# An order written out by hand, re-made: half-height products in one group, two spectra formed in other ways, convolution by row pairs

## The chip, the core and the metric

The kernel runs on one core of one Trainium2 chip. The core has a matrix engine (PE, with the loading of its stationary operand shown apart as PEld), three engines for element-wise work (DVE, ACT, POOL) and one that only starts transfers (SP). They run side by side, each through its own list of instructions in order, and wait for each other by semaphores. SP and POOL start nearly all transfers, so a transfer also waits for whatever stands ahead of it in their lists. The metric is the device time of one execution in microseconds; lower is better.

## The reference

Two layers follow each other on 2048 tokens of width 640, in bf16.

```
h  = x + q' * (irfft(rfft(kv) * rfft(ssm_k)) + kv * ssm_D)     # first 2048 samples of a length-4096 convolution
     q' = layernorm(x),  kv = v * (k filtered with 4 taps along the tokens)
h2 = h + (silu(n @ w_gate) * (n @ w_up)) @ w_down,   n = layernorm(h),  w_gate, w_up: 640 x 1728
```

So each channel is convolved with a filter as long as the sequence, and a gated feed-forward layer (FFN) follows. 1728 is 13 chunks of 128 and one chunk of 64.

## The kernel before

The 2048 tokens are cut into four blocks of 512 (block 0 to 3). A block is laid out with four tokens per partition: partition p holds tokens 4p to 4p+3, and "row r" is the 128 tokens 4p+r.

The long convolution is done block against block with transforms of length 1024. For each block j there is

- a short filter (`kv_of`): taps as diagonal matrices, multiplied on PE. For blocks 1 to 3, k lies in a buffer `T`, transposed by DMA and copied so that one product takes two taps (64 output columns each, 20 products for each row r, 80 for a block, line L648). The three copies inside `T` (`load_two`) are transfers and ACT copies. The result is multiplied by v to give kv.
- a spectrum X of kv and a spectrum G of the filter's block (`transform`, products at L375 with the basis `WF`; 128 x 320 each, two for a width of 640). The half of the frequencies comes from the even rows, the other from the odd rows: `hi = twice the even part - lo` is a subtraction on DVE (L410). In the form "four" (`SUM`) the rows are split once more, by n mod 4: half as many products, but more sums on DVE (L439, L443). In the form "direct" (`DIRECT`, only G of block 0) the difference is made on PE with a second, negated basis that is loaded into `tT` (`const_minus`).
- a window H from two neighbouring G (`window`, and `window_of` for the last block), the complex products X[i] * H[j-i] summed over i (`mac`: four multiplications and two additions for the first pair of a block, four and four for each further one; L719, L746, L747), and the way back (`inverse`, L823 to L858 on DVE, L878 on PE).
- two layer norms. `ln1` (of x) and the second norm take sums on ACT (L757, L796); the rest (`norm`: mean, variance, inverse root) is a run of tiny instructions, on POOL for `ln1` of every block and for the second norm of blocks 1 and 2, on DVE for the second norm of blocks 0 and 3. `h = x + (x-m)*s*y` is one fused instruction on DVE from PSUM (L892) and an addition (L905, or an accumulating transfer).
- the transposed rows hT for the FFN: on PE for block 0, by DMA from SP for blocks 1 to 3 (`turn_h`, L919).

The FFN of a block (`ffn`) has 27 products of 5 x 128x512 for gate and up (L1022, evicted by ACT at L1012 and L1014, multiplied on DVE at L1016, L1034 and L1039) and then, row by row, 14 chunks x 2 halves of 128x320 with `w_down` (L1110). The 14th chunk has only 64 features; it is padded with zeros to 128. Rows of blocks 0 to 2 are copied out of PSUM by ACT (L1116) and added to the output by a transfer; those of block 3 are added to h on DVE (L1125, L1127).

Additions of two big tiles can be done by DVE or by an accumulating transfer that POOL starts (`add_into`, L278). The names in `ADDLO`, `ADDWIN`, `ADDH`, `ADDP`, `ADDINV` say which.

Nothing of the sequence follows from loops. Every step is recorded as a numbered operation, and the list `ORDER` gives the order in which all operations are emitted; a negative number takes the operation's alternative engine. Buffers are taken from fixed pools in that order:

```python
SLOTS = {'S': 8, 'big': 12, 'kT': 0, 'tT': 1, 'row': 5, 'sg': 0, 'co': 2, 'ps': 4, 'sm': 6}
...
        for n in order:
            op = self.ops[n if n >= 0 else ~n]
            ...
            for b in op.bufs:
                if b.tag is not None and b.at is None:
                    b.at = idle[b.tag].pop(0)
```

There are thus four PSUM tiles (`ps`, two banks each) and twelve large tiles (`big`) for everything, the FFN's weights among it.

In the order before, the FFN of block j-1 fills PE while the convolution of block j keeps DVE busy; the FFN of block 3 stands alone at the end.

Of the kernel before, what the change touches and what calls it, by code (L numbers as in the profile page):

```python
# [17 lines left out]
D = 640  # L18
# [13 lines left out]
ADDLO = ('G1', 'G2', 'X1', 'X2', 'X3')  # L32
ADDMAC = ()
ADDWIN = (1,)
ADDH = (1, 2)
LEAD = {}
PAD = 16
DIRECT = ('G0',)
# [8 lines left out]
SUM = {'X3': 'four', 'i2': 'four', 'i3': 'four', 'G3': 'four'}  # L47
ADDP = {(1, 1): ((0, 1),)}
ADDINV = (2,)
# [9 lines left out]
KVPAIR = ()  # L59
DPOOL = False  # L60
# [54 lines left out]
def make_basis():  # L115
# [14 lines left out]
    minus = np.stack([(wf[:, r].astype(np.float32) * -2).astype(bf) for r in (1, 3)] + [-wi[:, :, r].reshape(P, 4 * P) for r in (1, 3)], axis=1)  # L130
    return wf.reshape(P, R, 4, P), wi, np.ascontiguousarray(minus)

class Buf:
# [76 lines left out]
def kernel(ctx: ExitStack, tc: tile.TileContext, A_q, A_k, A_v, A_shift_k, A_ssm_k, A_ssm_D, B_x,  # L213
# [493 lines left out]
    def mac(A, X, H, first, pieces=((0, 1),), adds=(), at=None):  # L707
# [26 lines left out]
        if first:  # L734
            return
# [595 lines left out]
```

## Time and profile before

| | us |
|---|---|
| median of 3 runs | 261.12 |
| lowest, highest | 260.46, 261.9 |
| span of the profiled execution, first to last instruction | 259.6 |
| PE busy, DVE busy, ACT busy, POOL busy | 251.3, 198.6, 180.0, 97.0 |
| granted TensorE clock | 1.0 throughout |
| moved by DMA | 45.38 MB |

For the profiled execution itself only its span is given; the runs' median lies 1.5 us above it. "Busy" is the time in which at least one instruction of the engine is under way. For PE this includes the time a product takes to leave the array, so back-to-back products count as one stretch. The start of one product to the start of the next is read from the chain or the timeline, where runs of equal products are merged with their count.

### The profile page before, as it was taken

The page shows a single profiled execution, that of the slowest core. Times are in us where ns is not written, and L with a number is a line of the kernel's source. Part 1 is how long each engine was busy: PE and PEld are TensorE (multiplying, and loading weights), DVE is VectorE, ACT ScalarE, POOL GpSimd, SP SyncE. Part 2 cuts the span into 40 slices and gives each one's busy share as a digit, 9 for nine tenths or more (in the row PEclk, how much of TensorE's full clock was granted, in tenths as well). Part 3 has the DMA queues.
Part 4 walks back from the last instruction along what each step waited for, and adds up shares of the span by engine and source line. Part 5 has one row for each costly group of instructions (what it writes and reads, how often), then busy time and mean ns, then how long its engine had stood idle before and what let it go on. Part 6 is the DMA issues. An engine that isn't in the chain of part 4 may idle for free.

```text
span 259.6 us, 4700 instructions
## 1 busy us (share of the span) xinstructions
PE 251.3 (97%) x1803; PEld 154.2 (59%) x1818; DVE 198.6 (77%) x259; ACT 180.0 (69%) x297; POOL 97.0 (37%) x115
## 2 busy tenths in 40 slices
PE   8999899999998999999999999999999999999994
PEld 7967577654654477754465477544456764444663
DVE  4679999999998999999999999999998200004403
ACT  2899999999998998569855985655497134637200
POOL 7961300008914199926117962240951022000000
PEclk9999999999999999999999999999999999999999
DMA  6997999979999998999997965994498546000002
GB/s 218 403 251 119 289 252 340 280 115 279 247 238 168 182 217 204 190 191 201 214 231 110 299 151 107 198 238 130 100 215 255 101 77 70 8 0 0 13 15 76
DMA packets 64752, 45.38 MB, mean 175 GB/s; under 512 B 31014, under 2 KB 60267, under 8 KB 64731
## 3 DMA queue, kind: packets, MB, share of 16 engines
q1 hardware_dynamic: 58896, 32.96, 51.1%
q0 software_dynamic: 5824, 12.13, 24.9%
q8 instruction: 14, 0.23, 0.4%
q14 instruction: 8, 0.06, 0.1%
q10 hardware_dynamic: 10, 0.01, 0.0%
HBM read 30.01 MB, written 4.59 MB: 133 GB/s over the span
## 4 chain that ended last, share of the span: by engine, by line
PE 78%; ACT 9%; DMA 6%; DVE 2%; issue 2%; SPq 1%; ACTq 0%; DVEq 0%
PE ps L1022 40%; PE ps L1110 23%; PE ps L375 10%; DMA big<-in_B_w_up_dram 4%; PE ps L878 3%; DMA big<-in_A_q_dram 3%; ACT T L565 2%; ACT big L364 1%; ACT S L364 1%; PE ps L648 1%; ACT row L757 1%; ACT big L664 1%; ACT big L473 1%; ACT tT L1014 1%; DVE row L892 1%
## 5 line engine op out<-in xcount | busy, mean ns | idle before, releaser
L1022 PE MATMUL ps<-big,big 128*128 128x512 bf16 x525 | 119.9, 379 | 1.7 <-DMA big<-in_B_w_up_dram 0.8
L1022 PEld LDWEIGHTS <-big 128*128 128x128 bf16 x540 | 52.5, 98 | 61.1 <-DMA big<-in_B_w_up_dram 1.3
L1110 PE MATMUL ps<-wd,tT 128*128 128x320 bf16 (+1 forms) x416 | 60.3, 299 | 0.0
L1110 PEld LDWEIGHTS <-tT 128*128 128x128 bf16 x416 | 40.7, 98 | 16.3
L1016 DVE TENSOR_TENSOR tT<-tT,co 128x2048 bf16<-128x2048 bf16 x12 | 14.5, 1219 | 34.4 <-ACT tT L1014 32.4
L375 PE MATMUL ps<-big,WF 128*128 128x320 bf16 x240 | 39.1, 299 | 1.3 <-ACT big L364 1.0
L1012 ACT CAST co<-ps 128x1024 bf16<-128x1024 f32 x24 | 24.2, 1011 | 17.3 <-PE ps L1022 16.8
L747 DVE TENSOR_TENSOR S<-S,big 128x2560 bf16<-128x2560 bf16 x23 | 34.3, 1492 | 1.2 <-DMA S<-big 0.5
L746 DVE TENSOR_TENSOR big<-S,S 128x2560 bf16<-128x2560 bf16 x23 | 34.1, 1485 | 0.2
L375 PEld LDWEIGHTS <-WF 128*128 128x128 bf16 x240 | 23.1, 97 | 12.8 <-issue 2.3
L1014 ACT ACTIVATE tT<-ps 128x1024 bf16<-128x1024 f32 x24 | 24.5, 1029 | 8.8 <-PE ps L1022 8.7
L757 ACT ACTIVATE row<-big 128x640 bf16<-128x640 bf16 x32 | 23.5, 742 | 1.8 <-DMA big<-in_A_q_dram 1.1
L807 ACT ACTIVATE row<-big,sm 128x640 bf16<-128x640 bf16 x23 | 20.3, 922 | 3.8 <-POOL sm L789 2.8
L1117 POOL DMA_DIRECT2D out_dram<-row x12 | 11.8, 1010 | 29.2 <-ACT row L1116 29.1
L364 ACT CAST S<-ps 128x320 bf16<-128x320 f32 (+1 forms) x36 | 19.4, 583 | 0.3
L1116 ACT CAST row<-ps 128x640 bf16<-128x640 f32 x12 | 8.1, 691 | 14.2 <-PE ps L1110 13.2
L364 ACT ACTIVATE big<-ps 128x640 bf16<-128x640 f32 (+1 forms) x24 | 15.6, 696 | 0.7 <-PE ps L375 0.7
L278 POOL DMA_DIRECT2D big<-row x8 | 7.0, 919 | 22.9 <-DVE row L892 22.9
L892 DVE SCALAR_TENSOR_TENSOR row<-row,ps 128x640 bf16<-128x640 bf16 x16 | 12.8, 815 | 1.1 <-PE ps L878 0.9
L278 POOL DMA_DIRECT2D S<-big x2 | 2.5, 1266 | 26.3 <-DVE S L719 19.1
L719 DVE TENSOR_TENSOR big<-S,S 128x2560 bf16<-128x2560 bf16 (+1 forms) x10 | 12.2, 1218 | 0.1
L959 POOL DMA_DIRECT2D big<-in_B_w_gate_dram x8 | 9.1, 1137 | 8.1 <-PE ps L1022 7.8
(110 smaller groups left out, 330.4 us busy)
## 6 DMA issues: line engine op xcount, KB each, us to landing
big<-in_B_w_up_dram SPq DMA_DIRECT2D x17, 320.0 KB, 5.1
big<-in_B_w_gate_dram SPq DMA_DIRECT2D x16, 320.0 KB, 4.7
big<-in_A_ssm_k_dram SPq DMA_DIRECT2D x4, 640.0 KB, 9.2
big<-in_A_q_dram SPq DMA_DIRECT2D x4, 640.0 KB, 7.6
big<-in_A_v_dram SPq DMA_DIRECT2D x4, 640.0 KB, 6.9
big<-in_B_w_gate_dram POOLq DMA_DIRECT2D x8, 320.0 KB, 7.2
big<-in_B_w_up_dram POOLq DMA_DIRECT2D x7, 320.0 KB, 6.7
wd<-in_B_w_down_dram SPq DMA_DIRECT2D x1, 2080.0 KB, 12.2
```

The lines of the kernel that those rows point to most:

```text
L364: (lambda: nc.scalar.activation(dst(), src(), ACT.Copy, scale=2.0)) if twice else (lambda: nc.scalar.copy(dst(), src())),
L375: nc.tensor.matmul(ap(ps)[:, h, 0:NH], w, ap(src)[:, r, h * NH:(h + 1) * NH], start=(first and i == 0), stop=(last and i == len(rs) - 1), ...
L746: nc.vector.tensor_mul(flat2(b), X.part(xs), H.part(hs))
L747: f(A.part(dst), A.part(dst), flat2(b))
L757: act(825, lambda r=r, junk=junk: nc.scalar.activation(ap(junk), ap(x)[:, r, :], ACT.Square, scale=D ** -0.5, accum_out=sm(s, 1)[:, r:r + ...
L807: nc.scalar.activation(ap(row), ap(x)[:, r, :], ACT.Identity, bias=sm(s, 5)[:, r:r + 1], scale=sm(s, 4)[:, r:r + 1])
L892: nc.vector.scalar_tensor_tensor(two(ap(t)), two(ap(t)), 1.0, half(ap(ps)), op0=ALU.mult, op1=ALU.mult, accum_out=sm(s, 0)[:, r:r + 1])
L1012: act(1010, lambda ps=ps: nc.scalar.copy(ap(co)[:, at:at + 2, :], ap(ps)), src, [(co, gi % 2)])
L1014: act(1010, lambda ps=ps: nc.scalar.activation(ap(tT)[:, c:c + 2, :], ap(ps), ACT.Silu), src, [done(range(c, c + 2), ROWS)])
L1016: dve(1220, lambda: nc.vector.tensor_mul(ap(tT)[:, c - 2:c + 2, :], ap(tT)[:, c - 2:c + 2, :], ap(co)), [co], [done(range(c - 2, c + 2), R ...
L1022: nc.tensor.matmul(ap(ps)[:, i, :], ap(w)[:, k, off:off + P], ap(hT)[:, k, :], start=(k == 0), stop=(k == KT - 1))
L1110: nc.tensor.matmul(ap(ps)[:, hf, to:to + n], t, ap(wd)[:, c, col + (hf - hs[0]) * NH:col + (hf - hs[0]) * NH + n], start=(c == order[0]), ...
```

## The change

Five things are changed, and `ORDER` is new as a whole.

1. The 14th chunk of the FFN is kept as 64 rows. Its activations of the rows 1 and 3 go to partitions 0 to 63 of `tail` and those of rows 0 and 2 to partitions 64 to 127; the last 64 rows of `w_down` are loaded twice. In `in_pairs` (which takes the place of the loop over rows) the products of the 14th chunk of all four rows (blocks 0 to 2) or of two rows (block 3) are emitted as one group, in turns from the lower and the upper half of the partitions. All rows of a group must have their PSUM tile open by then. The two memsets of zeros go; ACT's tail steps become 16 of 64x256 instead of 8 of 64x512.
2. X of block 2 is made in the form "four".
3. G of block 0 is made from partial sums like the others; the negated basis and its load of 512 KB go.
4. `by_rows`: the short filter of blocks 1 to 3 is made for two rows together (a, a+2). A pair of taps that both rows use is one product of 128 columns. Per block there are 16 products of 128 and 48 of 64 columns instead of 80 of 64, and three evictions (two of 1024, one of 512) instead of four of 640.
5. For block 0 (`MERGEH`), h is made with two fused instructions, `(x-m)*y` and `*s + x`, in place of ACT's normalised row, one fused instruction and an addition.

The lists that chose accumulating transfers are empty; which additions are transfers is now chosen by negative numbers in `ORDER` (`or_add`). 13 are: one in block 1's sums, one window, six of the eight additions of h in blocks 1 and 2, two halves of block 3's window, three in block 3's sums.

Read off the instruction lists of the two kernels: the multiplications and additions of `mac`, until now emitted as one operation, are separate, and other instructions stand between nearly all of them. On DVE, both window steps of block 1 stand ahead of the last normalised row of block 0. On POOL, the two copies inside `T` for block 1 stand ahead of block 0's `ln1`, behind which they stood. On SP, the filter block of block 2 is loaded ahead of the first copy inside `T`. The large products are the same in number: 540 of 128x512 and 448 with `w_down`. Three of block 3's sums are accumulating transfers started by POOL while DVE makes the last sums.

```diff
-ADDLO = ('G1', 'G2', 'X1', 'X2', 'X3')
+ADDLO = ()
-DIRECT = ('G0',)
+DIRECT = ()
-SUM = {'X3': 'four', 'i2': 'four', 'i3': 'four', 'G3': 'four'}
+SUM = {'X2': 'four', 'X3': 'four', 'i2': 'four', 'i3': 'four', 'G3': 'four'}
+KVTWO = True
+MERGEH = (0,)
+TAILPAIR = True
+TAILFOUR = (0, 1, 2)
...
+    def by_rows(kv, v):
...
+                for c in range(KT - 1):
+                    for b in range(2):
+                        o = ap(ps)[:, c // 2, (c % 2 * 2 + b) * P:(c % 2 * 2 + b + 1) * P]
+                        for q, at, p, n in ((0, a, 0, 2), (0, a - 2, 1, 1), (1, a + 2, 0, 1)):
+                            nc.tensor.matmul(o[:, q * H2:(q + n) * H2], win(b, c, at), tap(c, b, p, n), start=(n == 2), stop=(n == 1), skip_group_check=True)
...
-            def go(b=b, xs=xs, hs=hs, dst=dst, f=f):
-                nc.vector.tensor_mul(flat2(b), X.part(xs), H.part(hs))
-                f(A.part(dst), A.part(dst), flat2(b))
-            dve(3010, go, [X.at(xs), H.at(hs)], [b, A.at(dst)])
+            dve(1490, lambda b=b, xs=xs, hs=hs: nc.vector.tensor_mul(flat2(b), X.part(xs), H.part(hs)), [X.at(xs), H.at(hs)], [b], [A.b])
+            dve(1490, lambda b=b, dst=dst, f=f: f(A.part(dst), A.part(dst), flat2(b)), [b], [A.at(dst)])
+            if not (xs and hs):
+                or_add(lambda dst=dst: A.part(dst), lambda b=b: flat2(b))
...
+                if plan.block in MERGEH:
+                    def product(r=r, ps=ps, t=t):
+                        nc.vector.scalar_tensor_tensor(two(ap(t)), two(ap(x)[:, r, :]), sm(n1, 2)[:, r:r + 1], half(ap(ps)), op0=ALU.add, op1=ALU.mult)
+
+                    def total(r=r, t=t, s=s):
+                        nc.vector.scalar_tensor_tensor(ap(x)[:, r, :], ap(t), sm(n1, 4)[:, r:r + 1], ap(x)[:, r, :], op0=ALU.mult, op1=ALU.add,
+                                                       accum_out=sm(s, 0)[:, r:r + 1])
...
+    def in_pairs(j, tT, h, end, there, done, done_tail, behind, back):
...
+        def last_chunk(pair, parts, left):
+            def mm():
+                for hf, i, r in [(hf, i, r) for both in zip(pair[::2], pair[1::2]) for hf in range(2) for i, r in enumerate(both)]:
+                    ps, hs, n, col = [q for q in parts[r] if hf in q[1]][0]
+                    p0, at, col = 64 * i, ROWS.index(r) % 2 * P, col + (hf - hs[0]) * n
+                    product(ap(ps)[:, hf, 0:n], ap(tail)[p0:p0 + 64, at:at + P], ap(wd)[p0:p0 + 64, NC_FULL, col:col + n], start=False, stop=r != left)
...
+        for pair in [ROWS] if j in TAILFOUR else pairs:
+            parts = {}
+            for r in pair:
+                parts[r] = open_row(r)
+                for lo, hi in steps[:1] if r == pair[-1] else steps:
+                    chunks_of(r, parts[r], lo, hi, False)
+            last_chunk(pair if len(pair) == 2 else [r for p in pairs for r in p], parts, pair[-1])
+            for lo, hi in steps[1:]:
+                chunks_of(pair[-1], parts[pair[-1]], lo, hi, True)
...
-            load(64 * D * 2, 1280, lambda: nc.sync.dma_start(out=ap(wd)[0:64, NC_FULL, :], in_=B_w_down[NC_FULL * P:FF, :]), [(wd, 1)])
+            for i in range(2 if TAILPAIR else 1):
+                load(64 * D * 2, 1280, lambda i=i: nc.sync.dma_start(out=ap(wd)[64 * i:64 * i + 64, NC_FULL, :], in_=B_w_down[NC_FULL * P:FF, :]), [(wd, 1 + i)])
```

More of the change, by code (lines that the diff above doesn't have):

```diff
@@ L198, in schedule @@
                 op.eng, op.ns, op.fn = op.other
-                if op.rest:
-                    op.rest.fn = None
+                for left in op.rest:
+                    left.fn = None
             for b in op.bufs:
@@ L279, in add_into, with or_add @@
             out=to(), in_=what(), accum_op=ALU.add, max_dma_last_dim=2 * D * 2), r, w)
+    def or_add(to, what, n=R * D):
+        op = plan.ops[-1]
+        op.other = ("add", P * n * 2 / 1280 * plan.TOOK[1280] / 16 * 2.1, lambda: nc.gpsimd.dma_start(
+            out=to(), in_=what(), accum_op=ALU.add, max_dma_last_dim=2 * D * 2))
     def half(t):
@@ L539, in window_of @@
                 dve(820, first, [twice if h else lo, was], [to])
+                if not sin:
+                    or_add(lambda h=h: prev.part(1, h=h), lambda h=h: rows(twice if h else lo, 0), R * D // 2)
                 if h:
@@ L630, in kv_of @@
         kv = new("t4")
+        if two_taps and KVTWO:
+            by_rows(kv, v)
+            return kv
         for r in (0, 2, 1, 3) if plan.block in KVPAIR else range(R):
@@ L767, in fused @@
                 v.tensor_tensor(out, out, b, op=op1)
+        plan_block = plan.block
         def sm(s, i):
@@ L944, in load_w @@
             return (ws[0], 0), (ws[1], 0)
+        if (plan.block, gi) in KEEP:
+            return kept[gi]
         w = new("wgu")
@@ L961, in load_w, with open_row, product, chunks_of @@
         plan.name = was
-        return (w, 0), (w, 2 * P)
-    paired = []
+        kept[gi] = (w, 0), (w, 2 * P)
+        return kept[gi]
+    paired, kept = [], {}
+    def in_pairs(j, tT, h, end, there, done, done_tail, behind, back):
+        order = list(range(NC_FULL))
+        if back:
+            order.reverse()
+        cuts = [0, 5, 9, NC_FULL]
+        def open_row(r):
+            ps = new("ps_f")
+            if not (end and r == ROWS[-1]):
+                return [(ps, (0, 1), NH, 0)]
+            return [(ps, (0,), D - 2 * P, 0), (new("ps_f"), (1,), 2 * P, D - 2 * P)]
+        def product(to, t, w, **flags):
+            nc.tensor.matmul(to, t, w, skip_group_check=True, **flags)
+        def chunks_of(r, parts, lo, hi, closes):
+            at = ROWS.index(r) * P
+            for ps, hs, n, col in parts:
+                def mm(ps=ps, hs=hs, n=n, col=col):
+                    for c in order[lo:hi]:
+                        for i, hf in enumerate(hs):
+                            product(ap(ps)[:, hf, 0:n], ap(tT)[:, c, at:at + P], ap(wd)[:, c, col + i * n:col + i * n + n],
+                                    start=c == order[0], stop=closes and c == order[-1])
+                pe(136 * (hi - lo) * len(hs) * n // NH, mm, [wd, done(order[lo:hi], (r,))], [(ps, hf) for hf in hs]).deps.add(behind)
+        def last_chunk(pair, parts, left):
+            def mm():
+                for hf, i, r in [(hf, i, r) for both in zip(pair[::2], pair[1::2]) for hf in range(2) for i, r in enumerate(both)]:
+                    ps, hs, n, col = [q for q in parts[r] if hf in q[1]][0]
+                    p0, at, col = 64 * i, ROWS.index(r) % 2 * P, col + (hf - hs[0]) * n
+                    product(ap(ps)[:, hf, 0:n], ap(tail)[p0:p0 + 64, at:at + P], ap(wd)[p0:p0 + 64, NC_FULL, col:col + n], start=False, stop=r != left)
+            pe(165 + 165 * len(pair) // 2, mm, [wd, done_tail(pair)], [(ps, hf) for r in pair for ps, hs, n, col in parts[r] for hf in hs]).deps.add(behind)
+        steps = list(zip(cuts, cuts[1:]))
+        pairs = list(zip(*HALVES))
+        for pair in [ROWS] if j in TAILFOUR else pairs:
[7 more added lines that the diff above has]
+                chunks_of(pair[-1], parts[pair[-1]], lo, hi, True)
+            for r in pair:
+                o = new("o")
+                if not end:
+                    (ps, _, _, _), = parts[r]
+                    act(700, lambda ps=ps, o=o: nc.scalar.copy(two(ap(o)), half(ap(ps))), [ps], [o])
+                    plan.moved("add", MB / 4, 1280, lambda r=r, o=o: nc.gpsimd.dma_start(out=block(oo, j)[:, r, :], in_=ap(o), accum_op=ALU.add), [o], [(there, r)])
+                    continue
+                for ps, hs, n, lo in parts[r]:
+                    m = n * len(hs)
+                    def out_of(r=r, ps=ps, o=o, hs=hs, lo=lo, m=m):
+                        t = ap(h)[:, r, lo:lo + m]
+                        if len(hs) == 2:
+                            nc.vector.tensor_add(two(ap(o)), half(ap(ps)), two(t))
+                        else:
+                            nc.vector.tensor_add(ap(o)[:, lo:lo + m], ap(ps)[:, hs[0], 0:m], t)
+                    dve(160 + 1.03 * m, out_of, [(ps, hf) for hf in hs] + [(h, r)], [(o, (lo, m))])
+                    load(P * m * 2, 2 * m, lambda r=r, o=o, lo=lo, m=m: nc.sync.dma_start(out=block(oo, j)[:, r, lo:lo + m], in_=ap(o)[:, lo:lo + m]),
+                         [], [(o, (lo, m))])
@@ L1036, in odd_by_four @@
             last = whole(ps, 0, w, 2 * P)
+            if TAILPAIR:
+                n = BLK // 2
+                for i, rs in enumerate(HALVES):
+                    act(345, lambda ps=ps, i=i: nc.scalar.activation(ap(tail)[64 * i:64 * i + 64, :], ap(ps)[0:64, 0, i * n:(i + 1) * n], ACT.Silu),
+                        [(ps, 0)], [done_tail(rs)], [tT])
+                for i, rs in enumerate(HALVES):
+                    act(340, lambda ps=ps, i=i: nc.scalar.copy(ap(co)[64 * i:64 * i + 64, 1, 0:n], ap(ps)[64:P, 0, i * n:(i + 1) * n]),
+                        [(ps, 0)], [(co, (1, i))])
+                dve(250, lambda: nc.vector.tensor_mul(ap(tail), ap(tail), ap(co)[:, 1, 0:n]), [(co, (1, 0)), (co, (1, 1))], [done_tail(ROWS)], [tT])
+                return last
             act(600, lambda ps=ps: nc.scalar.activation(ap(tail)[0:64, :], ap(ps)[0:64, 0, :], ACT.Silu), [(ps, 0)], [done_tail(ROWS)], [tT])
@@ L1082, in ffn @@
             chunks((gi, gi + 1), first)
-        for gi in range(lead, NGRP - 1):
-            by_four(gi) if FFN4 else chunks((gi,), ROWS)
-        behind = odd_by_four() if FFN4 else odd_chunks()
+        back = any(b == j and gi == NGRP - 1 for b, gi in KEEP)
+        if back:
+            odd_by_four()
+            for gi in range(NGRP - 3, -1, -2):
+                by_four(gi)
+                behind = by_four(gi + 1)
+        else:
+            for gi in range(lead, NGRP - 1):
+                by_four(gi) if FFN4 else chunks((gi,), ROWS)
+            behind = odd_by_four() if FFN4 else odd_chunks()
         for gi in range(0, lead, 2):
             behind = chunks((gi, gi + 1), then)
-        for r in ROWS:
+        if TAILPAIR:
+            in_pairs(j, tT, h, end, there, done, done_tail, behind, back)
+        for r in () if TAILPAIR else ROWS:
             ps = new("ps_f")
             order = list(range(lead * 2, NCH)) + list(range(lead * 2))
+            if back:
+                order.reverse()
             last = end and r == ROWS[-1]
@@ L1204 @@
     if DIRECT:
-        load(P * R * 4 * P * 2, 4096, lambda: nc.sync.dma_start(out=ap(minus)[:, 0:4, :], in_=minus_h.ap()), [minus])
+        act(910, lambda: nc.scalar.activation(ap(minus)[:, 0:2, :].rearrange("p a (c q) -> p a c q", c=4), ap(WF)[:, 1::2], ACT.Copy, scale=-2.0), [WF], [(minus, "f")])
+        plan.ops[-1].other = ("dve", 350, lambda: nc.vector.tensor_scalar(
+            ap(minus)[:, 0:2, :].rearrange("p a (c q) -> p a c q", c=4), ap(WF)[:, 1::2], -2.0, None, op0=ALU.mult))
     first("Ld")
```

101 lines of the change are left out of this document (76 added, 25 removed), and 75 rows, old and new, of the table ORDER.

## The prediction

> **What bounds the kernel now.** I read the page's shares first (PE leads, DVE follows), then the windows cut at the four FFN starts, then the chain, then DVE and SP just before the last FFN.
>
> ```profile
> 0.00:49.70 49.70, 46.63 (x507) 36.39 (x508) 41.84 (x94) 42.92 (x93) 19.42 (x44) 1.00 1.00 265
> 49.70:113.80 64.10, 63.00 (x441) 38.10 (x444) 62.46 (x55) 57.28 (x90) 34.94 (x30) 1.00 1.01 210
> 113.80:165.20 51.40, 51.14 (x356) 30.01 (x359) 50.71 (x54) 39.16 (x61) 25.18 (x25) 1.00 0.87 187
> 165.20:211.70 46.50, 46.34 (x261) 25.73 (x263) 35.92 (x49) 24.47 (x36) 14.84 (x14) 1.00 0.71 170
> 211.70:256.10 44.40, 44.19 (x244) 23.95 (x245) 7.29 (x10) 16.14 (x19) 2.58 (x3) 1.00 0.14 23
> ```
>
> Columns: window, its length, busy PE, PEld, DVE, ACT, POOL, clock, DMA share, GB/s. From 49.7 to 256.1 us PE is idle for 1.7 us in all. But DVE is full too, until near 200 us: 62.5 of 64.1 us, then 50.7 of 51.4. So two resources run out together, and what counts is where they meet, the start of the last FFN.
>
> ```profile
> 196.48 15.21 PE ps L1110 x112
> 211.70 0.22 PE ps L1022
> ...
> 256.06 0.02 issue
> 256.09 0.42 DVE row L1127
> ```
>
> ```profile
> 201.16 0.16 DVE L789 TENSOR_TENSOR sm<-sm 128x4 f32<-128x4 f32 x1
> 201.71 5.17 SPq L919 DMA_TRANSPOSE big<-row  x4
> L919 SPq DMA_TRANSPOSE big<-row x12: 1198/1228/1439, 101.6 to 205.7; - x12
> DMA to landing us min/median/max: 2.6/2.6/4.9
> ```
>
> In the chain PE goes from the down product of block 2 straight into FFN 3 at 211.7. The other way in: DVE ends block 3's norm at 201.3, SP issues four transposes from 201.71, the last at 205.7, landing 2.6 later, at 208.3. So DVE's path has a slack of only 3.4 us. **PE work taken out ahead of FFN 3 is worth at most 3.4 us unless DVE's path gets shorter as well.** After FFN 3's start, 44.4 us of PE and 3.5 us of output follow in any case.
>
> **PE's path.** Paces come from runs in the chain:
>
> ```profile
> 20.84 0.28 PE ps L471 x5
> 105.13 0.54 PE ps L375 x4
> 136.87 0.66 PE ps L648 x20
> 154.03 11.14 PE ps L1110 x82
> ```
>
> That is 0.136 us for 320 columns, 0.056 for 128, 0.033 for 64.
>
> - Spectra: 256 products become 224. Sixteen of these belong to X of block 2, behind FFN 0's start: 16 x 0.136 = 2.2 us, all on PE's path. The other sixteen are G of block 0, ahead of 49.7 us, where PE is idle for 3.1 us anyway; they count only as far as that phase gets shorter.
> - Short filter: 80 x 0.033 = 2.64 us a block become 16 x 0.056 + 48 x 0.033 = 2.48: 0.16 a block, 0.3 us for blocks 2 and 3.
> - Moved: with the new order two groups of four spectrum products (ps tiles of L375) stand behind the first FFN product instead of five: 3 x 0.54 = 1.6 us have gone to the front.
> - Half-height products: 32 in number before and after. If the two halves of the array work at once, each pair takes the time of one and 16 x 0.136 = 2.2 us go, 1.6 of them ahead of FFN 3. If not, nothing goes. No 64-row product is in the trace.
>
> ```profile
> L1110 PE MATMUL ps<-wd,tT 128*128 128x320 bf16 x390 | 56.7, 299 | 0.0
> ```
>
> One product lasts 0.299 us but the next starts 0.136 later; 0.163 us of each is the array running empty under its successor. If entering or leaving the half-height form exposed that, 5 groups x 2 x 0.163 = 1.6 us would be lost. So the edit lies between -2.2 and +1.6 us; I take -1.4 in all, -1.1 of it ahead of FFN 3, nearer to full overlap, because two different halves have no common cell. The Trainium skill ("TensorEngine Tiling (Array Packing)", Key Properties) has both: tiles work independently, and changing the tiling mode drains the engine. By the drain alone the sum would be +1.6, by independence alone -2.2; the trace shows neither.
>
> Such a group has all four PSUM tiles open, so spectrum products stand still until ACT copies rows out. The sixteen products of the fourth row that follow (2.2 us) cover most of these copies; I count nothing and leave what is left over to the range.
>
> - Front: FFN 0 needs block 0's normalised rows from DVE. In the new list both window steps (1.48 us each) stand ahead of the last of these rows, 2.8 us; the first product of spectra (DVE at 22.50 before) should come 1 to 2 us earlier, since G no longer waits for the second basis and is half done before kv. A delay of FFN 0 of 0 to 3 us; I take 1.5.
>
> PE is then ready for FFN 3 at 211.7 - 2.2 - 0.3 - 1.6 - 1.1 + 1.5 = **208.0**.
>
> **DVE's path.**
>
> ```profile
> 22.50 0.82 DVE L719 TENSOR_TENSOR S<-S,S 128x1280 bf16<-128x1280 bf16 x1
> ...
> 35.76 0.89 DVE L905 TENSOR_TENSOR big<-big,row 128x640 bf16<-128x640 bf16 x2
> ...
> 61.62 1.48 DVE L746 TENSOR_TENSOR big<-S,S 128x2560 bf16<-128x2560 bf16 x1
> 63.14 1.49 DVE L747 TENSOR_TENSOR S<-S,big 128x2560 bf16<-128x2560 bf16 x1
> 64.55 1.48 DVE L746 TENSOR_TENSOR big<-S,S 128x2560 bf16<-128x2560 bf16 x1
> ```
>
> ```profile
> L892 DVE SCALAR_TENSOR_TENSOR row<-row,ps 128x640 bf16<-128x640 bf16 x16 | 12.8, 815 | 1.1 <-PE ps L878 0.9 <-ACT row L807 0.2
> L473 DVE COPY big<-ps 128x640 bf16<-128x640 bf16 x5 | 2.3, 486 | 1.1 <-PE ps L471 1.1
> L804 DVE TENSOR_SCALAR row<-big,sm 128x640 bf16<-128x640 bf16 x9 | 3.7, 439 | 0.0
> L905 DVE TENSOR_TENSOR big<-big,row 128x640 bf16<-128x640 bf16 x8 | 3.7, 488 | 0.1
> ```
>
> Added: two subtractions for G of block 0 at 0.82 (1.6); X of block 2 in four parts, 1.48 becoming 2 x 0.82 + 2 x 1.48 (3.1); sums that were transfers and are now DVE's, X of block 3, the way back of block 2 (2 x 1.48) and two additions of h (1.0); block 0's h, four of 0.82 and 0.49 becoming eight of 0.82 (1.3). Together 10.0. Removed: the adds of products that are transfers are four instead of one (4.4); two half-size window adds (1.6); four normalised rows at 0.44 (1.8); four copies of G at 0.49 (1.9); in narrower evictions, the tail and the wide kv products I estimate 1 to 2. Together 10.7 to 11.7. By durations that is 1 us less; but neighbours overlap by some 0.07 us (1.48 lasts, 1.41 to the next), and part lies behind the norm, so I take 0 to -1 and count 0.
>
> Separating multiply and add does count: from a multiply to the add that needs it DVE takes 1.52, from an add to an independent multiply 1.41. Of 21 such adds 19 now have something in between: 19 x 0.11 = 2.1 us. Against it: two waits that the order adds.
>
> ```profile
> 15.63 0.20 POOL L775 TENSOR_TENSOR sm<-sm 128x4 f32<-128x4 f32 x1 [1.45 <-ACT row L796]
> 18.14 0.20 POOL L789 TENSOR_TENSOR sm<-sm 128x4 f32<-128x4 f32 x1
> 27.73 1.51 POOL L563 DMA_DIRECT2D T<-T  x2 [7.06 <-ACT big L473]
> 60.29 2.87 POOL L775 TENSOR_TENSOR sm<-sm 128x4 f32<-128x4 f32 x1
> 68.55 0.47 POOL L789 TENSOR_TENSOR sm<-sm 128x4 f32<-128x4 f32 x1
> big<-in_A_ssm_k_dram SPq DMA_DIRECT2D x4, 640.0 KB, 9.2
> S<-big POOLq DMA_DIRECT2D x2, 640.0 KB, 8.3
> L959 POOL DMA_DIRECT2D big<-in_B_w_gate_dram x8 | 9.1, 1137 | 8.1 <-PE ps L1022 7.8 <-issue 0.2
> ```
>
> - Block 0's `ln1` on POOL was done at 18.3 us; it now stands behind the two copies inside `T`, which were issued at 27.7. The run takes 2.7 us where DVE has gaps and 8.7 us where it is full, so it ends between 32 and 38. The Trainium skill ("SBUF — State Buffer", the shared port pair) has DVE operations with two SBUF inputs lock out POOL's reads, which is the longer of the two. Who waits: DVE's second fused instruction of block 0, which takes the place of the addition that stood at 35.76, and all behind it. Zero to 3.5 us; I take 1.5, less 0.8 for the earlier start of the products.
> - Three adds of block 3 as transfers, 8.3 us each to landing; the last has some 9.6 us of DVE work between its product and the first subtraction of the way back. I take 0.7.
>
> hT of block 3 lands at 208.3 - 2.1 + 1.5 - 0.8 + 0.7 = **207.6**.
>
> **Sum.** FFN 3 starts at 208.0 instead of 211.7: -3.7. Its two half-height groups: -0.3. The last output is a whole row instead of 256 columns: 0.82 instead of 0.42 on DVE, and
>
> ```profile
> out_dram<-row SPq DMA_DIRECT2D x3, 160.0 KB, 1.8
> out_dram<-row SPq DMA_DIRECT2D x1, 64.0 KB, 1.5
> ```
>
> together +0.7. Net -3.3 on the span of 259.6. The runs' median lies 1.5 above that span, and I take this as unchanged: 261.1 - 3.3 = **257.8 us**. DMA moves 0.5 MB less and ACT does about 2 us more in all; neither is on these paths.
>
> **Rivals.**
>
> 1. Both paths shorter. No delay in front, full overlap of the half-height pairs, no wait for transfers: PE ready at 211.7 - 2.2 - 0.3 - 1.6 - 1.6 = 206.0, DVE's path 205.2; 5.7 + 0.5 - 0.7 = 5.5 us less, 255.6. For it: 19 pairs are plainly separated. Against: the front's window steps.
> 2. DVE's path eats it. The three accumulating transfers of block 3 share POOL's list with weight loads that take 1.1 us each to start; three of them ahead make the way back wait 3.5 us, hT lands at 211.1, and the time is 261.1 - 0.6 - 0.3 + 0.7 = 260.9. For it: 8.3 us against 9.6 leaves little. The same figure results if the new order simply has other stalls of 3 us.
> 3. Slower: the front breaks on POOL. The first copy inside `T` now has the load of block 2's filter ahead of it (640 KB, 9.2 us to landing). If the copies can start only near 34 us and the `ln1` behind them takes its 8.7, DVE stands until 43 and FFN 0 starts 7 us late; PE is ready at 213.5 and the time is 261.1 + 1.8 - 0.3 + 0.7 = 263.3. It decides when block 0's `ln1` ends after 41 us. Against it: the load is in flight at the same time as the copy, not wholly before it.
>
> **Numbers.** Forecast 0.50, both shorter 0.17, eaten up 0.15, slower 0.18. 0.5% (1.3 us) is about what a measurement of this kernel can tell. Faster 0.67, same 0.15, slower 0.18. The first case runs from 256 to 259.7 with the front at 0 to 3, half-height products at their ends and transfers at 0 to 2; with the faster case from 254.0 (front 1 us early) and the eaten-up one to 262.4, the range is 254.0 to 262.4.
>
> **What would show it.** Right: L1022 of block 0 starts at 50 to 53, of block 3 near 208, directly behind both the last L1110-type product and the last transpose; tail products start less than 0.1 us apart; DVE's multiplies and adds follow each other at 1.41. Wrong: a stall of over 2 us of DVE behind POOL near 35 us or behind a transfer near 183; tail products at 0.136 or more; PE idle for more than 2 us between the FFNs.

## The result

The changed kernel takes 263.1 us (median of 18 runs, 261.3 to 265.3), the kernel before 260.9 (18 runs, 260.1 to 262.7). The ratio is 1.0082 with a 95% interval of 1.0054 to 1.0109: slower by 0.8%, where 257.8 was forecast. The profiled execution took 263.3 with a span of 261.6.

The stages of the profile after, cut at the four FFN starts as before (window, its length, busy PE, PEld, DVE, ACT, POOL, clock, DMA share, GB/s):

```profile
0.00:52.51 52.51, 47.70 (x486) 37.16 (x487) 44.02 (x89) 45.49 (x96) 18.54 (x42) 1.00 0.99 258
52.51:115.86 63.35, 59.50 (x401) 34.73 (x400) 59.09 (x54) 53.95 (x83) 34.27 (x25) 1.00 0.88 185
115.86:166.56 50.70, 50.70 (x344) 29.02 (x341) 49.56 (x51) 39.80 (x62) 23.52 (x26) 1.00 0.92 203
166.56:213.25 46.69, 46.62 (x267) 25.39 (x265) 36.85 (x50) 30.82 (x51) 18.83 (x20) 1.00 0.85 189
213.25:257.69 44.44, 44.40 (x249) 23.34 (x246) 6.75 (x10) 14.84 (x19) 4.27 (x5) 1.00 0.18 30
```

The last FFN starts at 213.25 instead of 211.7, and its length is 44.4 as before. Apart from FFN 0's start, 2.8 us late where 1.5 was forecast, the damage is in one stage. From 115.86 on PE has no idle time to speak of (50.70 of 50.70, 46.62 of 46.69). But between FFN 0 and FFN 1 PE is busy for only 59.5 of 63.35 us, where it was 63.0 of 64.1: it has less work there, and stands still for longer. The timeline of PE shows the holes, in the last column with what ended them:

```profile
79.42 2.33 PE L955 MATMUL ps<-S,WI 128*128 128x320 bf16 x16 [1.50 <-ACT big L703]
...
95.27 0.43 PE L387 MATMUL ps<-big,WF 128*128 128x320 bf16 x2 [1.24 <-ACT co L1169]
96.19 1.52 PE L1072 MATMUL ps<-wd,tT 128*128 128x320 bf16 x10 [0.49 <-ACT tT L1171]
```

With one of 0.61 at 83.86, left out here, that is 3.8 us. Each hole ends with an ACT instruction that waits for nothing special itself: ACT is late as a whole. The chain says why (start, length, what):

```profile
60.38 15.01 POOL sm L850
...
77.98 0.92 ACT row L882
...
85.20 8.27 DMA big<-row
...
93.49 0.83 ACT row L828 x2
94.32 0.90 ACT co L1169
```

A POOL instruction on 128x4 numbers, the first of block 1's `ln1` run, takes 15 us (the chain counts it from the end of the instruction ahead of it, the timeline from its own start). Behind it wait ACT's normalised rows (L882), DVE's fused instruction (L979), the accumulating transfers of h (L291, 8.27 us) and ACT's squares of h (L828); in ACT's list stand, between and behind these, the evictions of kv (L703) and of FFN 0 (L1169), for which PE waits. POOL's timeline beside DVE's:

```profile
59.91 15.46 POOL L850 TENSOR_TENSOR sm<-sm 128x4 f32<-128x4 f32 x1
...
77.47 0.48 POOL L864 TENSOR_TENSOR sm<-sm 128x4 f32<-128x4 f32 x1
```

```profile
60.08 1.49 DVE L788 TENSOR_TENSOR S<-S,big 128x2560 bf16<-128x2560 bf16 x1
61.48 5.70 DVE L816 TENSOR_TENSOR big<-S,S 128x2560 bf16<-128x2560 bf16 x4
67.08 5.70 DVE L817 TENSOR_TENSOR S<-S,big 128x2560 bf16<-128x2560 bf16 x4
72.69 1.23 DVE L1173 TENSOR_TENSOR tT<-tT,co 128x2048 bf16<-128x2048 bf16 x1
73.82 1.50 DVE L898 TENSOR_TENSOR big<-S 128x2560 bf16<-128x2560 bf16 x1
75.78 0.70 DVE L705 TENSOR_TENSOR big<-big,big 128x1024 bf16<-128x1024 bf16 x1 [0.46 <-ACT big L703]
```

From 60.08 to 75.3 DVE goes from one two-input instruction to the next, each 1.40 after the last (1.13 behind the shorter L1173). L850 ends at 75.37, in DVE's first idle moment. Before, the same instruction (L775 at 60.29, 2.87 us) ended at 63.16, where DVE stood between a multiplication and the addition that needs it. This suggests that those small waits, which the change took out, let POOL work; the experiments test it. The second instruction of the run, in the kernel before, did not need such a wait:

```profile
63.24 1.45 POOL L785 TENSOR_TENSOR sm<-sm 128x4 f32<-128x4 f32 x1
```

It ended at 64.69, just after DVE had gone on at 64.55 to a multiplication that waited for nothing.

The Trainium skill ("SBUF — State Buffer", "SBUF: two separate sides") has a DVE instruction with two SBUF inputs hold the port that POOL reads through, for the whole instruction, with the other side blocked. The trace agrees with the block, but not with its length: it lasted across eleven DVE instructions, not one.

### The profile page after: what moved, and what is told of

Read it like the earlier page. It is cut to its first block, busy times and chain, and to the rows that moved or that the text cites. A ratio compares the mean times of both kernels' runs of the same rounds, so it can differ in the third digit from the quotient of the medians.

```text
span 261.6 us, 4550 instructions
## 1 busy us (share of the span) xinstructions
PE 248.9 (95%) x1738; PEld 149.6 (57%) x1738; DVE 197.1 (75%) x251; ACT 184.9 (71%) x308; POOL 99.4 (38%) x114
## 2 busy tenths in 40 slices
DMA packets 65278, 45.91 MB, mean 175 GB/s; under 512 B 31029, under 2 KB 60410, under 8 KB 65258
## 4 chain that ended last, share of the span: by engine, by line
PE 67%; ACT 9%; DVE 8%; POOL 7%; DMA 5%; issue 2%; DVEq 0%; POOLq 0%
PE ps L1179 31%; PE ps L1072 23%; POOL sm L850 6%; PE ps L387 5%; DMA big<-row 3%; PE ps L955 2%; ACT row L882 2%; DMA big<-in_A_ssm_k_dram 2%; PE ps L660 2%; ACT S L376 1%; DVE big L969 1%; ACT big L487 1%; ACT big L376 1%; DVE big L788 1%; DVE S L534 1%
## 5 line engine op out<-in xcount | busy, mean ns | idle before, releaser
L1072 PE MATMUL ps<-wd,tT 128*128 128x320 bf16 (+2 forms) x416 | 59.2, 299 | 0.5 <-ACT tT L1171 0.5
L1173 DVE TENSOR_TENSOR tT<-tT,co 128x2048 bf16<-128x2048 bf16 x12 | 14.7, 1223 | 38.9 <-ACT tT L1171 20.8
L387 PE MATMUL ps<-big,WF 128*128 128x320 bf16 x224 | 37.3, 298 | 2.7 <-ACT co L1169 1.2
L1169 ACT CAST co<-ps 128x1024 bf16<-128x1024 f32 x24 | 23.9, 1009 | 18.7 <-PE ps L1179 18.6
L816 DVE TENSOR_TENSOR big<-S,S 128x2560 bf16<-128x2560 bf16 x24 | 34.8, 1487 | 0.2
L817 DVE TENSOR_TENSOR S<-S,big 128x2560 bf16<-128x2560 bf16 x21 | 30.8, 1488 | 0.1
L387 PEld LDWEIGHTS <-WF 128*128 128x128 bf16 x224 | 21.3, 97 | 14.1 <-issue 4.9
L828 ACT ACTIVATE row<-big 128x640 bf16<-128x640 bf16 x32 | 23.5, 738 | 4.2 <-DMA big<-row 2.3
L882 ACT ACTIVATE row<-big,sm 128x640 bf16<-128x640 bf16 x23 | 19.7, 914 | 3.7 <-POOL sm L864 2.2
L850 POOL TENSOR_TENSOR sm<-sm 128x4 f32<-128x4 f32 x6 | 19.9, 3318 | 5.2 <-ACT row L871 5.0
L376 ACT CAST S<-ps 128x640 bf16<-128x640 f32 (+1 forms) x28 | 15.6, 613 | 2.0 <-PE ps L387 2.0
L291 POOL DMA_DIRECT2D S<-big x6 | 7.2, 1206 | 19.0 <-DVE big L816 5.9
L955 PEld LDWEIGHTS <-WI 128*128 128x128 bf16 x96 | 9.4, 98 | 6.7 <-issue 1.7
L788 DVE TENSOR_TENSOR S<-S,S 128x2560 bf16<-128x2560 bf16 (+1 forms) x10 | 12.2, 1219 | 0.0
```

What stands on the lines that cost most here:

```text
L376: (lambda: nc.scalar.activation(dst(), src(), ACT.Copy, scale=2.0)) if twice else (lambda: nc.scalar.copy(dst(), src())),
L387: nc.tensor.matmul(ap(ps)[:, h, 0:NH], w, ap(src)[:, r, h * NH:(h + 1) * NH], start=(first and i == 0), stop=(last and i == len(rs) - 1), ...
L788: return lambda: f(*(x() for x in args))
L816: dve(1490, lambda b=b, xs=xs, hs=hs: nc.vector.tensor_mul(flat2(b), X.part(xs), H.part(hs)), [X.at(xs), H.at(hs)], [b], [A.b])
L817: dve(1490, lambda b=b, dst=dst, f=f: f(A.part(dst), A.part(dst), flat2(b)), [b], [A.at(dst)])
L828: act(825, lambda r=r, junk=junk: nc.scalar.activation(ap(junk), ap(x)[:, r, :], ACT.Square, scale=D ** -0.5, accum_out=sm(s, 1)[:, r:r + ...
```

## The experiments

Theory A is this: L850 starves because multiplications and additions no longer wait for each other. Theory B, the rival: FFN 0's late start (52.5 instead of 49.7) is the loss, and the stalls are only DVE's load.

**Waits put back.** Four tiny copies on DVE, each of the result just made:

```diff
             if op.fn:
                 op.fn()
+            if op.n in (263, 261, 265, 267):
+                nc.vector.tensor_copy(ap(gap), place["big"][op.bufs[-1].at][:, 0:4])
```

> The changed kernel with four more instructions: behind each of the four multiplications of block 1's second pair DVE copies four columns of what it has just made (128x4) into an unused tile, so that DVE has to wait for its own result four times between 61 and 69 us. Theory A (the first instruction of block 1's ln1 run on POOL, L850, can't finish while DVE's multiplications and additions follow each other without a gap): L850 takes under 4 us instead of 15.5, the run ends near 70 instead of 78, PE's idle time between FFN 0 and FFN 1 falls from 3.8 to under 1.5 us, and the kernel gets 2 to 3 us faster although DVE does more: 260.5. Theory B (the loss is the late start of FFN 0 alone, 52.5 instead of 49.7, and the stalls are a mere consequence of DVE's load): L850 still ends at DVE's next stall near 75, and the time goes up by the four instructions, to 263 to 264.

Measured 258.7 us (258.5 to 259.8), ratio to the kernel before 0.9912 (0.9881 to 0.9942). With four more instructions the changed kernel is 4.4 us faster, and faster than the kernel before. POOL's timeline, and PE's at the last FFN:

```profile
58.88 3.11 POOL L850 TENSOR_TENSOR sm<-sm 128x4 f32<-128x4 f32 x1
...
67.72 0.67 POOL L864 TENSOR_TENSOR sm<-sm 128x4 f32<-128x4 f32 x1
```

```profile
208.28 28.22 PE L1179 MATMUL ps<-big,big 128*128 128x512 bf16 x127
```

The run ends at 68.4 instead of 77.95, PE's timeline between FFN 0 and FFN 1 has one hole left, of 0.26 us, and FFN 3 starts at 208.28. The gain was larger than theory A's 2 to 3 us: from FFN 0 to FFN 3 the profiles differ by 3.9 us, and FFN 0 itself starts 1.0 earlier, which goes with the quicker of two kinds of start (last section).

**The run on DVE.** One name: `LN1DVE = (1,)` instead of `()`.

> The changed kernel with block 1's ln1 run (mean, variance, inverse root) on DVE instead of POOL, at the same place in the order: nine tiny instructions, some 1.8 us of DVE by the second norm of block 0. Theory A (the run starves on POOL): s of block 1 is there by 68 instead of 78, PE's idle time between FFN 0 and FFN 1 falls from 3.8 to under 1 us, FFN 3 starts near 210.3, 260.3 us in all. Theory B (late start of FFN 0 alone): DVE is full there and gets 1.8 us more, so the time goes up, 263 to 265.

Measured 259.7 (259.1 to 260.7), ratio 0.9939 (0.9914 to 0.9963). PE's three holes there are 0.27, 0.74 and 0.21 us, FFN 3 starts at 209.2. Two different edits, both without a starved POOL instruction, take away the same stall; theory B predicted a loss from each.

**One wait, and copies without a wait.** The first keeps one copy, behind operation 263; the second keeps four, which read the constant `ident` and so wait for nothing.

> The changed kernel with only the first of the four small copies of the run before (behind L816's first multiplication of block 1's second pair). Theory A1 (each instruction of the POOL run needs a gap of its own): L850 ends near 62 like with four copies, but L860 behind it then lasts until DVE's next stall near 75, the run ends near 78, and the time is that of the changed kernel, 262 to 264. Theory A2 (one gap lets POOL in, and what follows runs freely): the run ends by 68, 258.7 us as with four.

> As the run with four small copies of 128x4, but they read the constant identity tile instead of what the multiplication has just made, so DVE doesn't wait for its own result. Theory A3 (POOL gets in while DVE waits): L850 lasts until 75 again, 263 us. Theory A4 (an instruction of DVE that reads only one tile is enough): L850 takes about 3 us, the run ends by 69, and the time is 258.7 as with the dependent copies.

Measured 259.1 (0.9925, 0.9896 to 0.9953) and 258.9 (0.9917, 0.9891 to 0.9942). POOL with one dependent copy, then with four independent ones:

```profile
60.02 3.11 POOL L850 TENSOR_TENSOR sm<-sm 128x4 f32<-128x4 f32 x1
...
68.45 0.47 POOL L864 TENSOR_TENSOR sm<-sm 128x4 f32<-128x4 f32 x1
```

```profile
60.01 3.12 POOL L850 TENSOR_TENSOR sm<-sm 128x4 f32<-128x4 f32 x1
...
68.48 7.28 POOL L864 TENSOR_TENSOR sm<-sm 128x4 f32<-128x4 f32 x1
```

and DVE's next wait in the second of these runs:

```profile
75.89 0.69 DVE L705 TENSOR_TENSOR big<-big,big 128x1024 bf16<-128x1024 bf16 x1 [0.19 <-ACT big L703]
```

A1 fell: after one wait the other four instructions of the run got in too, between DVE instructions that follow each other without a wait. A3 fell as well: an instruction that reads one tile and waits for nothing is enough. But neither A2 nor A4 is the whole rule. With the independent copies the fifth instruction was caught again, for 7.3 us, until DVE waited at 75.8. So a POOL instruction can be held over many DVE instructions or slip in between two of them; what decides it stays open. That run ended at 75.8 and cost nothing, the changed kernel's at 77.95 cost 3.8 us of PE: the slack lies between.

**The same run, one place earlier in POOL's list.** The run is moved ahead of the accumulating transfer behind which it stood (operation 277 ahead of 260).

> The changed kernel, with block 1's ln1 run on POOL one place earlier, ahead of the accumulating transfer of block 1's sums; nothing else is moved. Its sums are there near 55.5 us. If DVE's unbroken row of instructions is what holds POOL, L850 starts at 55 to 56 and still ends only at DVE's next stall; the transfer behind it is issued late, the addition that needs its result waits, and that wait is DVE's next stall: near 67 instead of 75, then over 6 us long. Time 262 to 268. If the place behind the transfer was what held POOL, L850 takes under 3 us, the run ends by 62, and the time is 258.7.

Measured 268.5 (267.3 to 268.8), ratio 1.0253 (1.0207 to 1.0300). POOL, DVE and PE:

```profile
54.83 12.85 POOL L850 TENSOR_TENSOR sm<-sm 128x4 f32<-128x4 f32 x1 [2.33 <-ACT row L871]
```

```profile
77.28 4.29 DVE L817 TENSOR_TENSOR S<-S,big 128x2560 bf16<-128x2560 bf16 x3 [9.65 <-DMA S<-big]
```

```profile
84.19 2.31 PE L955 MATMUL ps<-big,WI 128*128 128x320 bf16 x8 [8.29 <-DVE big L898]
86.29 3.84 PE L955 MATMUL ps<-S,WI 128*128 128x320 bf16 x16
```

As theory A said: L850 is caught at 54.8 and freed at 67.68, when DVE runs into the result of the transfer that stands behind it. The transfer is issued only at 70.0, and DVE stands 9.65 us. The time is 0.5 above the 262 to 268 that were expected; PE's hole of 8.29 us is followed by eight products at half pace (2.10 us), which the expectation did not count.

**The reverse, in the kernel before.** Block 1's second pair with its multiplications and additions set apart:

```diff
-            b = new("scr")
+            b, apart = new("scr"), at == (1, 1)
+            late = late if xs or hs else []
...
-            def go(b=b, xs=xs, hs=hs, dst=dst, f=f):
-                nc.vector.tensor_mul(flat2(b), X.part(xs), H.part(hs))
-                f(A.part(dst), A.part(dst), flat2(b))
-            dve(3010, go, [X.at(xs), H.at(hs)], [b, A.at(dst)])
+            add = lambda b=b, dst=dst, f=f: f(A.part(dst), A.part(dst), flat2(b))
+            dve(3010, lambda b=b, xs=xs, hs=hs, now=late + [add] * (not apart or xs > hs): [nc.vector.tensor_mul(flat2(b), X.part(xs), H.part(hs))] + [a() for a in now], [X.at(xs), H.at(hs)], [b, A.at(dst)])
+            late = [add] if apart else []
```

> The kernel before, with the multiplications and additions of block 1's second pair set apart as in the changed kernel, and nothing else moved (in DVE's list: multiply, multiply, add, multiply, add, add). Theory A (starvation by the separation alone): the first instruction of block 1's ln1 run on POOL (L775) takes over 7 us instead of 2.9, the run ends after 73 instead of 69, PE's idle time between FFN 0 and FFN 1 grows from 0.8 to 2 to 4 us, and the kernel gets 1 to 3 us slower: 262 to 264. Rival (the stall of the changed kernel comes from something else in its order, a transfer or a place in POOL's list): L775 as before, and the time falls by the three short waits, 0.3 us, to 260.7.

Measured 261.6 (260.3 to 263.3), ratio 1.0022 (0.9999 to 1.0046). The first POOL instruction took twice as long:

```profile
60.70 5.67 POOL L775 TENSOR_TENSOR sm<-sm 128x4 f32<-128x4 f32 x1
```

It ended at 66.37, in the first gap left on DVE, 0.04 us between an addition and the multiplication that starts at 66.35 (why DVE waits there, the trace does not say). The run ended at 71.1, which is early enough: PE's idle time stayed at 1.0 us. POOL is held for as long as DVE leaves no gap, as theory A said, but the predicted 1 to 3 us don't show. By time this run is inconclusive: the separation of one pair alone doesn't make the kernel before measurably slower.

**The front.** Both window steps moved behind block 0's last normalised row (operations 227 and 228 behind the alternative of 175), alone and with the run on DVE.

> The changed kernel with both window steps of block 1 (L531, L534) behind the last normalised row of block 0 instead of ahead of it, nothing else moved. FFN 0 should start 2.8 us earlier, near 49.7. Theory A (what binds in the stage of FFN 0 is the starved run on POOL and ACT's rows behind it, which come from DVE's stream and not from FFN 0's start): PE only waits longer, its idle time between FFN 0 and FFN 1 grows from 3.8 to over 6 us, and the time stays at 262.5 to 263.5. Theory B (late start alone): everything follows by 2.8 us, 260.3.

> The two edits together: block 1's ln1 run on DVE, and the window steps of block 1 behind the last normalised row of block 0. Theory A: PE's path is 2.8 + 3.1 us shorter and ready for FFN 3 near 207.4, DVE's path near 208; together 257.7 us, faster than the kernel before by 3. Theory B: as with the window steps alone, 260.3, plus up to 1.8 for the run on DVE.

Measured 265.9 (265.3 to 266.9; 1.0183, 1.0150 to 1.0216) and 261.8 (260.1 to 263.9; 1.0008, 0.9977 to 1.0038). Both theories were wrong here. PE and POOL with the windows moved:

```profile
51.39 1.24 PE L1179 MATMUL ps<-big,big 128*128 128x512 bf16 x4
...
81.63 4.43 PE L955 MATMUL ps<-S,WI 128*128 128x320 bf16 x16 [4.84 <-ACT big L703]
85.85 1.58 PE L955 MATMUL ps<-big,WI 128*128 128x320 bf16 x8
```

```profile
60.07 18.07 POOL L850 TENSOR_TENSOR sm<-sm 128x4 f32<-128x4 f32 x1
```

FFN 0 starts at 51.39, where the run with the four copies, which left the windows in place, had 51.48: their place doesn't set it. In the changed order they fill the time in which DVE waits for ACT's squares and for kv (0.51 and 0.54 us, now idle). PE takes up the first rows at 46.92 instead of 47.26, and the last rows at 49.56 instead of 49.66, behind four spectrum products that wait 0.48 us for an eviction by ACT in both runs. So moving the windows wins nothing in front, and behind it block 1's run still starves (18.07 us). PE's hole grows to 4.84 us, and behind it sixteen products take 4.22 us, where the run with four copies has 2.19.

**Half-height products.** On top of the four copies, the products of a group first all from the lower half and then all from the upper half; and, in another run, all eight on the lower half, which takes the 14th chunk of rows 0 and 2 from the wrong rows.

```diff
-                for hf, i, r in [(hf, i, r) for both in zip(pair[::2], pair[1::2]) for hf in range(2) for i, r in enumerate(both)]:
+                for hf, i, r in [(hf, i, r) for i in range(2) for r in pair[i::2] for hf in range(2)]:
```

```diff
-                    p0, at, col = 64 * i, ROWS.index(r) % 2 * P, col + (hf - hs[0]) * n
+                    p0, at, col = 0, ROWS.index(r) % 2 * P, col + (hf - hs[0]) * n
```

> The changed kernel with the four small copies, and with the half-height products of a group in another order: all from the lower half of the partitions, then all from the upper half, instead of in turns. If the short group time (0.65 us for eight) comes from two halves of the array working at once, a group of eight takes near 1.0 us, FFN 3 starts 1.1 us later (three groups), and the time rises from 258.7 to about 260. If half-height products are short by themselves, nothing changes.

> The changed kernel with the four small copies; all half-height products now read partitions 0 to 63 of tail and w_down, also those that belong to partitions 64 to 127, so the 14th chunk of rows 0 and 2 is taken from the wrong rows. If two different halves of the array working at once make the group short (0.66 us for eight, in turns or not), a group of eight on one half takes about 1.1 us, and the time rises by 1.3, to about 260. If a half-height product is short by itself, the group stays at 0.66 and the time at 258.7 to 259.

Measured 259.7 (0.9935, 0.9913 to 0.9958) and 261.7 (1.0012, 0.9986 to 1.0038). One group in each, with the product that follows it; the difference of the two starts is the group's time:

```profile
105.06 0.73 PE L1072 MATMUL ps<-wd,tail 64*128 64x320 bf16 x8
105.72 1.26 PE L1072 MATMUL ps<-wd,tT 128*128 128x320 bf16 x8
```

```profile
104.49 1.26 PE L1072 MATMUL ps<-wd,tail 64*128 64x320 bf16 x8
105.68 1.26 PE L1072 MATMUL ps<-wd,tT 128*128 128x320 bf16 x8
```

The group takes 0.66 us without turns, 1.19 on one half. The first expectation, 1.0 us without turns if the halves work at once, was wrong: the order within the group doesn't matter. The second was right: a half-height product is not short by itself, so the two halves do work at once. On one half a group takes longer than eight full-height products (1.09). By time neither run is as clean. The runs without turns lie in two clusters, 258.6 to 258.9 and 259.6 to 260.1, as far apart as the two kinds of start in the last section. The run on one half is 3.0 above the run with four copies, not 1.3: three groups of eight and two groups of four (0.65 us each instead of 0.38) make 3 x 0.53 + 2 x 0.27 = 2.1 of it, and its profile has the slower start.

**The start.** Six more warm-up products (22 instead of 16 in the second set) on top of the four copies.

> The changed kernel with the four small copies, and with 22 instead of 16 warm-up products of 128 columns in PE's second set, so that PE is busy until the first load lands near 5.7 us. In some executions the first 20 transposes (L485) take 1.3 us and in others 2.3, and all that follows is 1.1 us earlier or later. If PE's idle time of 0.3 to 1.0 us ahead of them decides that, all executions now take 1.3, and the runs gather near 258.6 instead of 258.5 to 259.8. If not, the spread stays, and the median is 258.7 to 259.2.

Measured 258.95 (258.6 to 259.5), ratio 0.9905 (0.9875 to 0.9935). The first twenty transposes took 1.97 us in its profile, and the spread stays: the warm-up products don't settle it, and nothing is won.

## Why the prediction failed

**The step that failed** is the sentence "Separating multiply and add does count", with its gain of 19 x 0.11 = 2.1 us for DVE. The 0.11 us were real: in the changed kernel DVE's instructions follow each other at 1.40. But the waits had a user, for which the sum has no term. I had costed a POOL run in a stretch where DVE is full at 8.7 us, from a row taken in the old, gapped order, and applied it to block 0's `ln1`, which the diff moves. Block 1's `ln1`, which the diff doesn't move, I didn't cost again in the new order; it took 18.0 us, from 59.91 to 77.95, and PE stood still for 3.8 us behind it. One of the prediction's own signs of being wrong, PE idle for more than 2 us between the FFNs, is what came. A step has to be priced anew when its surroundings change, just as when it is moved itself.

With the starvation gone the rest of the sum holds to about 1 us. The run with four copies has FFN 0 at 51.48 (forecast 49.7 + 1.5 = 51.2), FFN 3 at 208.28 (forecast 208.0) and a span of 256.6 (forecast 259.6 - 3.3 = 256.3). That close a match is partly luck: its profile has the quicker start, and the run with four independent copies, with the slower one, has 52.62, 209.05 and 257.4.

Point by point:

- Spectra and their move: between the starts of FFN 0 and FFN 3, 72 products instead of 100 in PE's timeline, 28 x 0.136 = 3.8 us, as forecast (2.2 + 1.6).
- Half-height products, -1.4: a group of eight takes 0.65 us in the changed kernel and one of four 0.38, where full height would take 1.09 and 0.54; 3 x 0.44 + 2 x 0.16 = 1.6 us less. The value near full overlap was right. FFN 3 as a whole is not shorter, though: its -0.3 isn't seen.

```profile
108.66 0.72 PE L1072 MATMUL ps<-wd,tail 64*128 64x320 bf16 x8
109.31 1.26 PE L1072 MATMUL ps<-wd,tT 128*128 128x320 bf16 x8
```

- The front, +1.5: FFN 0 at 52.5, but 51.3 to 51.6 in executions with the quicker of the two kinds of start that the last section shows. The reason given, the window steps ahead of the last row, was wrong; with them behind it FFN 0 starts no earlier, so that the 1.5 comes near the 1.6 to 1.9 of these executions is luck. What does set it was not tested; the traces point to the first normalised row and to ACT's evictions.
- Block 0's `ln1` behind the copies: it ended at 32.0, ahead of DVE's first fused instruction at 35.1. So the third rival did not happen: its sign, this `ln1` ending after 41, fails, and FFN 0 is 2.8 us late instead of 7. That its 263.3 lies beside the measured 263.1 is luck. Only a part of it came true, in block 1: a POOL run held up by a full DVE, and the fused instructions behind it.

```profile
31.49 0.54 POOL L864 TENSOR_TENSOR sm<-sm 128x4 f32<-128x4 f32 x1
```

- DVE's path: SP's transposes for block 3 start at 203.89, not near 201, the waits of DVE in the stage of FFN 0 handed on. With the four copies they start at 198.92, so hT lands near 205.5 (forecast 207.6): block 3's accumulating transfers, for which I had put 0.7, cost nothing: DVE waits for no transfer from 160 to 205. The slack of DVE's path, which the prediction had at 0.4, is 2.8.

```profile
203.89 5.17 SPq L1008 DMA_TRANSPOSE big<-row  x4
```

- The output, +0.7: from the last addition's start to the end of the span 3.9 us instead of 3.5.
- Off the paths: DMA moves 45.91 MB, 0.5 more and not 0.5 less, and ACT does 4.9 us more, not 2. Neither explains the loss, since the run with four copies keeps both.

Together: forecast -3.3, measured +2.2 by the medians. The run with four copies puts 4.4 of these 5.5 us down to the starved run and what followed from it. Its own median stands 0.9 above the forecast, 0.6 of it because its runs lie 2.1 above the span instead of 1.5.

## What to carry to other kernels

An engine's small waits can be somebody else's only opening: before filling them, list what POOL has to do in that stretch, and give it an opening (here a copy of 128x4 on DVE was enough) or move the work to DVE, where nine tiny instructions cost 1.8 us. A price measured in the old order holds only for the old neighbours, so reprice what stands beside the edit, not just what it moves. And look for a long bar on a tiny instruction: 128x4 numbers that take 15 us are waiting, whatever the profile calls busy.

## What the runs showed of the hardware

POOL's hold was not one instruction long but up to 18.1 us, and it is counted as busy time. In these runs a copy of 128x4 on DVE let the held instruction through, whether or not the copy waited for anything (3.11 and 3.12 us instead of 15.46). It is not a sure cure: with the four independent copies the last of the five POOL instructions was held for 7.28 us.

PE went to half speed after a stall of 4.84 us: sixteen products of 320 columns took 4.22 us instead of 2.19, with a granted clock of 0.50 from 81.6 to 85.8, and the mean clock of that run is 0.987. After 8.29 us it did the same (0.50 from 84.1 to 88.0). After the changed kernel's single stalls of 1.5 us and less the clock stays at 1.00 in its profile. The Trainium skill ("TensorE: Matmul & The Clock Gate", "What's actually happening") gives an idle window of about 3.4 us for it, which lies between the stalls that had an effect here and those that had none; the rows pin it no closer. Five of the changed kernel's 18 runs have a mean clock of 0.994, and all five are above 264.6 us; that their stall was long enough for the half speed is a conclusion, since only one execution was traced.

The start comes in two kinds, too. The same twenty transposes take 1.3 us in some executions and 2.3 in others, with the stages behind them 1.1 us later; here the run with four copies and the changed kernel:

```profile
5.83 1.31 PE L485 MATMUL ps<-ident,big 128*128 128x128 bf16 x20 [1.04 <-DMA big<-in_A_ssm_k_dram]
```

```profile
5.71 2.32 PE L485 MATMUL ps<-ident,big 128*128 128x128 bf16 x20 [0.35 <-DMA big<-in_A_ssm_k_dram]
```

In the slower kind the twenty products start 0.106 us apart (5.71 to 7.83), in the quicker kind near the 0.056 of 128 columns elsewhere. That is half pace, though the profile's clock column reads 1.00 there. So about 1.1 of the 2.8 us by which FFN 0 is late in the profile after varies from execution to execution. Whether the change brought the slower kind along is open: the profile before and that of its variant with the pair set apart show the quicker pace (15 transposes in 1.0 us). What decides between them was not found; more warm-up products did not.
